# Attention in front of a Fourier mixer and an MLP: the product with V in 64-column halves, and the softmax's sums as a product of their own

## The chip, the cores and the metric

The kernel runs on one core of one Trainium2 chip. The metric is the device time of one execution in microseconds (us). The core has five engines that run side by side, each through its own instructions in order: TensorE (PE, matrix products), VectorE (DVE), ScalarE (ACT), GpSimd (POOL) and SyncE (SP, which here only issues DMA transfers).

## The reference

Eight batches, eight heads, 576 positions, head dimension 64, all in float32. Attention with a causal mask and a bias from cumulated sums comes first; its output goes, per batch as a 576 x 512 matrix, through a real part of a two-dimensional Fourier transform, a layer norm and an MLP of width 2048.

```python
scores = scale * (q @ k.T); bias = -(cum[:, None] - cum[None, :])
scores = where(causal, -1e9, scores + minimum(bias, 0)); scores -= max(scores)
attn = exp(scores); attn = attn / (sum(attn) + 1e-9)
x = attn @ v                       # per head: 576 x 576 times 576 x 64
u = x + real(fft(fft(x, axis=seq), axis=d_model))
un = (u - mean(u)) / sqrt(var(u) + 1e-6)
out = u + relu(un @ w_ch1) @ w_ch2
```

## The kernel before

Work goes in 32 **pairs** of heads (`NP`; four pairs make a batch). For pair `i` the function `maxes` finds the row maxima (products `pm`, line 459), `scores` forms transposed scores in PSUM (`ps`, lines 491 and 492: two products, high and low parts) and lets ACT write `P = exp(...)` to SBUF (line 495), after which POOL zeroes the masked corners (`affine_select`, lines 498 and 501). `P` of one head is a 128 x 1984 tile in five chunks of keys (`CH`, `POFF`): chunk 0 has 576 queries, chunk 1 has 448, and so on down to 64, because queries ahead of a key are masked.

`av` multiplies by V (line 523). Its operands are plain float32, not the one-pass `float32r` form that all other products but the transposes of `pmt` (line 471) use. Each head has two tiles of output columns, `pavA` (queries 0 to 255) and `pavB` (256 to 575), of 2 and 5 matmuls. The stationary operand is 128 columns wide: 64 columns of V of this head and 64 columns of ones, so 64 output rows are the head's result and the others the softmax's sums. ACT copies results to `x` (name `stage`) and the second head's sums to a row of `rows`; two DMAs per pair bring the sums to a tile `sums`. `recip` takes their reciprocals, writes them to DRAM (`rd`) and reads them back spread over partitions (`rb`); `finish` multiplies `x` by them. `recip` and `finish` of a pair are called an iteration after its `av`, except for the last pair.

The order is written by hand: in iteration `i`, `weave` mixes generators, always advancing the one whose yielded costs are the smallest share of its total. `av(i - 1)` (total `AV`), `maxes(i + 1)`, `low(i + 1)`, `high(i + 2)`, `scores(i)`, the Fourier products of the batch before (`pzs`, `pzc`, `pyc`, `pys`) and weight conversion are so interleaved. On PE this order is kept exactly. PSUM tiles of `maxes`, `av` and the transposes share five buffers of one tag. After the attention (line 622) come the last Fourier products and the MLP (`mlp_tile`, lines 183 to 198).

Of the kernel before, what the change touches and what calls it, by code (L numbers as in the profile page):

```python
# [8 lines left out]
F32 = mybir.dt.float32  # L9
# [10 lines left out]
S = 576  # L20
# [15 lines left out]
CH = [(0, 0, 576, 0), (128, 128, 448, 128), (256, 256, 320, 256), (384, 320, 256, 384), (448, 320, 256, 512)]  # L36
POFF = [0, 576, 1152, 1728, 1920]
# [4 lines left out]
def fused_kernel(ctx, tc, qkT, vA, sP, wP, tabD, tabS, corr, out):  # L42
    nc = tc.nc
# [4 lines left out]
    const = ctx.enter_context(tc.tile_pool(name="const", bufs=1))  # L48
# [6 lines left out]
    wD = dram.tile([NF, 128, 1024], F32, name="wD")  # L55
    uD = dram.tile([4, 128, NT], F32, name="uD")

    ident = const.tile([128, 128], F32, name="ident")
    make_identity(nc, ident)
    ones = const.tile([128, 128], F32R, name="ones")  # L60
# [40 lines left out]
    def load_w(pool, f):  # L101

        wh = pool.tile([128, 1024], F32R, tag=f"wh{f}", name=f"wh{f}")
        wl = pool.tile([128, 1024], F32R, tag=f"wl{f}", name=f"wl{f}")
        W[f] = (wh, wl)
        if f < NC:
            nc.sync.dma_start(out=wl.bitcast(F32), in_=wD[f])
        n = 512 if f < NC else WC
        for x in range(1024 // n):
            xs = slice(n * x, n * x + n)  # L110
            m = wl[:, xs].bitcast(F32) if f < NC else (yield from rounded(stage, f, x, nstage))
            nc.scalar.copy(wh[:, xs], m)  # L112
            yield 0.2 * n / 512
            (nc.vector if x * n < 512 else nc.gpsimd).tensor_sub(wl[:, xs], m, wh[:, xs].bitcast(F32))  # L114
            yield 0.2 * n / 512
# [101 lines left out]
    fft = fft_ctx.enter_context(tc.tile_pool(name="fft", bufs=1, side="right"))  # L217
# [7 lines left out]
    Aw = fft.tile([128, 577], F32, name="Aw")  # L225
    ZB = min(4, NB)
    z256 = [fft.tile([97, 3, ZB], F32R, name=f"z256{i}") for i in range(2)]
    rows = fft.tile([96, S], F32, name="rows")
    x256 = rows[:ZB]
    nc.vector.memset(Aw[:, 576:577], 0.0)  # L230

    def load_tables():
# [113 lines left out]
    attb = attb_ctx.enter_context(tc.tile_pool(name="attb", bufs=1, side="right"))  # L346
    psm = attb_ctx.enter_context(tc.tile_pool(name="psm", bufs=5, space=PSUM))
# [6 lines left out]
    cumD = dram.tile([3, 2, R, S], F32, name="cumD")  # L354
    cw = attb.tile([128, PW], F32, tag="P", name="cw", bufs=4)
    sp, zero, cum = (cw[:R, x * S:(x + 1) * S] for x in range(3))
    cumhl = attb.tile([128, PW], F32R, tag="P", name="cumhl", bufs=4)
    cw2 = attb.tile([128, PW], F32, tag="P", name="cw2", bufs=4)
    nc.sync.dma_start(out=sp, in_=sP)
# [63 lines left out]
    def low(i):  # L423

        st = sts[i]
        qk, qy, ky = st["qk"], st["qy"], st["ky"]
        pool = att if (NP - 1 - i) % 2 == 0 else atop
        q1 = pool.tile([128, 2, S], F32R, tag="q1", name="q1")
        k1 = pool.tile([128, 2, S], F32R, tag="k1", name="k1")
        nc.sync.dma_start(out=q1[0:64].bitcast(F32), in_=qy[64:128, :, 0:S].bitcast(F32))  # L430
        nc.sync.dma_start(out=k1[64:128].bitcast(F32), in_=ky[64:128].bitcast(F32))
        st.update(q1=q1, k1=k1)
        yield 1.0
        for h in range(2):
            nc.vector.tensor_sub(k1[0:64, h], qk[64:128, h], ky[64:128, h].bitcast(F32))
            yield 1.0
        for h in range(2):
            nc.gpsimd.tensor_sub(q1[64:128, h], qk[0:64, h], q1[0:64, h].bitcast(F32))  # L438
            yield 1.0
        va = attb.tile([128, 5, 192], F32, tag="va", name="va", bufs=2)  # L440
        nc.sync.dma_start(out=va, in_=vA[st["b"], :, :, st["j"]])
        st["va"] = va

# [35 lines left out]
    def scores(i):  # L479
        st = sts[i]  # L480
        qy, ky, q1, k1 = st["qy"], st["ky"], st["q1"], st["k1"]
        st["P"] = []
        for h in range(2):
            P = attb.tile([128, PW], F32, tag="P", name="P", bufs=4)
            st["P"].append(P)
            for c, (k0, q0, nq, qk) in enumerate(CH):
# [14 lines left out]
                        nc.gpsimd.affine_select(out=d5, in_=d5, pattern=[[1, 64]], compare_op=ALU.is_ge, fill=0.0, base=64, channel_multiplier=-1)  # L501
                    yield 2 * n / 2.4

    AV = 2 * 2700

    def av(i):
        st = sts[i]
        va = st["va"]
        x = attb.tile([128, S], F32, tag="stage", name="stage", bufs=3)
        r1 = rows[32 + 32 * (i % 2):33 + 32 * (i % 2)]  # L510
        sums = attb.tile([32, 36], F32, tag="sums", name="sums", bufs=2)
        for h in range(2):
            P = st["P"][h]
            vs = slice(64 * h, 64 * h + 128)
            for lo, n, tg in ((0, 256, "A"), (256, 320, "B")):
                p = psm.tile([128, 512], F32, tag="m", name="pav" + tg, bufs=5)
                cs = [c for c in range(5) if CH[c][3] < lo + n]
                for c in cs:
                    qk = CH[c][3]
                    a = max(lo, qk)  # L520
                    o = POFF[c] + a - qk
                    w = lo + n - a
                    nc.tensor.matmul(p[:, a - lo:n], va[:, c, vs], P[:, o:o + w], start=c == 0, stop=c == cs[-1])  # L523
                    if c == cs[-1]:
                        if h:
                            nc.scalar.copy(r1[:, lo:lo + n], p[0:1, :n])
                            nc.scalar.copy(x[64:128, lo:lo + n], p[64:128, :n])  # L527
                        else:
                            nc.scalar.copy(x[:, lo:lo + n], p[:, :n])
                    yield 4 * w / 2.4  # L530

            nc.sync.dma_start(out=sums[16 * h:16 * h + 16], in_=r1 if h else x[64:65])
        st.update(x=x, sums=sums)

    def recip(i):
# [29 lines left out]
    def call(fn, *args):  # L565
        yield 1.0
        fn(*args)
# [3 lines left out]
    weave([high(0), 1])  # L571
    cum_rows()
    weave([low(0), 1], [high(1), 1], [maxes(0), 1.0])
    weave([low(1), 1], [high(2), 1], [maxes(1), 1.0])
    mixing = None
    weights = convert_w(attb, 0, NC, 1)
# [8 lines left out]
    for i in range(NP):  # L585
# [3 lines left out]
        if i >= 1:  # L589
            streams.append([av(i - 1), AV * (0.95 if i % 4 == 1 else 1.0)])  # L590
        if 2 <= i + 1 < NP:
            streams.append([maxes(i + 1), MAXES / 0.7])
            streams.append([later(low(i + 1), i % 4 == 0), (6, 7, 4, 3)[i % 4]])
# [26 lines left out]
        if i >= 7 and i % 4 == 3:  # L620
# [5 lines left out]
    w0 = ctx.enter_context(pool("w0"))  # L626
    stage, nstage = attb, 1
    weave([later(call(recip, NP - 2), 2), 10], [later(call(finish, NP - 2), 4), 10], [av(NP - 1), AV], [mixing, FOURIER * 0.1], [norm, 6 * 0.4],
          [chain(weights, *[load_w(w0, f) for f in range(N0)]), 4 * N0 * 0.7 + 1])
    recip(NP - 1)  # L630
# [56 lines left out]
def chain(*gens):  # L687
    for g in gens:
        yield from g
# [6 lines left out]
def later(gen, n):  # L696
    for _ in range(n):
        yield 1.0
    yield from gen


def weave(*streams):

    for _ in mixed(*streams):
        pass
# [47 lines left out]
def _perm():  # L753
    import numpy as np

    p = np.arange(128)
    t2 = 512 - p
    t2[0] = 256
    return np.concatenate([p, 128 + p, t2, 384 - p])


def _layout(inputs):
    import numpy as np

    slots = [0, 1, 2, 3, 7, 6, 5, 4]
    perm = _perm()
    q, k, v, s = (inputs[n] for n in ("q", "k", "v", "s"))
    nb = q.shape[0]
    vs = v[:, slots].copy()
    vs[:, 4:] = vs[:, 4:, :, ::-1]  # L770
    vp = np.zeros((nb, NH, 640, HD), np.float32)
    vp[:, :, :S] = vs
    vp = vp.reshape(nb, 4, 2, 5, 128, HD)
    vA = np.ones((nb, 128, 5, 4, 192), np.float32)
    vA[..., 0:64] = vp[:, :, 0].transpose(0, 3, 2, 1, 4)
    vA[..., 128:192] = vp[:, :, 1].transpose(0, 3, 2, 1, 4)
    vA[:, 64:, 4] = vA[:, :64, 4]
    vA[:, :64, 4] = 0.0
    w1 = inputs["moe_w_ch1"][perm].reshape(4, 128, NF, 128)
    w2 = inputs["moe_w_ch2"][:, perm].reshape(NF, 128, DM)  # L780
    wP = np.concatenate([w1.transpose(2, 1, 0, 3).reshape(NF, 128, DM), w2], 2)
    wP = np.ascontiguousarray(wP).view(np.int64)
    tabD, tabS, corr = _tables()
    arrays = {
        "qkT": np.stack([a[:, slots].reshape(nb, 4, 2, S, HD).transpose(0, 1, 4, 2, 3) for a in (q, k)], 2).reshape(nb, 4, 128, 2, S),
        "vA": vA,
        "sP": s[:, slots].reshape(nb * NH, S),
        "wP": wP, "tabD": tabD, "tabS": tabS, "corr": corr,
    }
    return {n: np.ascontiguousarray(a) for n, a in arrays.items()}  # L790
# [22 lines left out]
```

## Time and profile before

| | us |
|---|---|
| three timed runs | 1425.22, 1425.87, 1433.48 (median 1425.87) |
| span of the profiled execution, first to last instruction | 1424.4 |
| PE, share of that span with a matmul under way | 1305.1 (92%) |
| DVE, ACT, POOL busy | 745.7, 539.3, 561.6 |

The profile is of one execution; its span stands 1.5 us below the median of the timed runs. A matmul's recorded duration includes its way through the array and overlaps that of the next, so starts, not durations, give its pace. One float32 product of line 523 makes two recorded matmuls, each with a weight load of its own (PEld).

### The profile page before, as it was taken

The numbers are of one execution on the slowest core, as the hardware profiler recorded it, in microseconds if no ns is written. First come the engines' busy times: TensorE is split into PE (matmuls) and PEld (weight loads), VectorE is DVE, ScalarE is ACT, GpSimd is POOL, SyncE is SP. The second block draws the span as 40 slices with busy tenths as digits, with TensorE's granted clock in tenths as the row PEclk, the third lists the DMA queues.
The fourth block names the chain that finished last, engine by engine and source line by source line (L and its number), as shares of the span: only waits on it lengthen the run. The fifth ranks groups of instructions, "written<-read, shape, count | busy, mean of one in ns | idle before, by whom it ended". The sixth has DMA issues, their size and how long they took to land.

```text
span 1424.4 us, 17997 instructions
## 1 busy us (share of the span) xinstructions
PE 1305.1 (92%) x6190; PEld 1068.7 (75%) x6190; DVE 745.7 (52%) x1684; ACT 539.3 (38%) x1211; POOL 561.6 (39%) x543
## 2 busy tenths in 40 slices
PE   4887979897988887997899999999999999999998
PEld 3766868686777676775688888888888888888886
DVE  6667677877777788799833233222332223322212
ACT  4775756676665656344321121211212112121110
POOL 6445465656546566565720402204022040123300
PEclk9998999999999997999899999999999999999999
DMA  8555556565655555433200000000000000000000
GB/s 214 156 159 144 163 149 180 158 168 159 159 161 144 166 149 163 162 123 121 79 8 30 31 30 15 15 30 31 30 15 15 30 30 30 15 16 0 30 0 30
DMA packets 78230, 125.05 MB, mean 88 GB/s; under 512 B 11256, under 2 KB 36249, under 8 KB 78139
## 3 DMA queue, kind: packets, MB, share of 16 engines
q1 hardware_dynamic: 75627, 119.83, 28.4%
q0 software_dynamic: 1696, 2.50, 0.9%
q10 hardware_dynamic: 816, 1.57, 0.3%
q8 instruction: 49, 0.80, 0.2%
q14 instruction: 42, 0.34, 0.1%
HBM read 76.85 MB, written 23.07 MB: 70 GB/s over the span
## 4 chain that ended last, share of the span: by engine, by line
PE 51%; DVE 7%; POOL 2%; DMA 1%; issue 1%; ACT 1%; SPq 0%; DVEq 0%; POOLq 0%; ACTq 0%
PE h L183 25%; PE acc L198 8%; PE acc L196 8%; PE acc L197 8%; POOL we L89 1%; DVE wm L88 1%; DVE we L83 1%; DVE wm L85 1%; DVE we L87 1%; DVE wl L114 1%; ACT wh L112 1%; DMA wl<-wD 0%; POOL wl L114 0%; DVE ucl L148 0%; DVE zl L188 0%
## 5 line engine op out<-in xcount | busy, mean ns | idle before, releaser
L188 DVE SCALAR_TENSOR_TENSOR zl<-h,zh 128x512 fp32r<-128x512 f32 x144 | 98.6, 686 | 405.5 <-ACT zh L187 405.4
L187 ACT ACTIVATE zh<-h 128x512 fp32r<-128x512 f32 x144 | 85.9, 596 | 530.1 <-PE h L183 530.1
L198 PE MATMUL acc<-zl,wh 128*128 128x512 f32 x576 | 227.5, 396 | 4.9 <-DVE zl L188 4.9
L196 PE MATMUL acc<-zh,wh 128*128 128x512 f32 x576 | 227.6, 395 | 1.0 <-ACT zh L187 1.0
L197 PE MATMUL acc<-zh,wl 128*128 128x512 f32 x576 | 226.8, 394 | 0.0
L523 PE MATMUL pavB<-P,va 128*128 128x320 f32 (+2 forms) x640 | 189.1, 389 | 9.5 <-ACT stage L527 8.9
L459 PE MATMUL pm<-KQ 128*128 128x256 f32 (+3 forms) x384 | 156.5, 427 | 44.4 <-DVE Mx L466 23.1
L495 ACT ACTIVATE P<-ps 128x320 f32<-128x320 f32 (+4 forms) x384 | 145.9, 393 | 110.5 <-PE ps L492 106.8
L491 PE MATMUL ps<-KQ 128*128 128x256 f32 (+2 forms) x384 | 154.1, 404 | 24.4 <-ACT P L495 14.0
L183 PE MATMUL h<-uch,wh 128*128 128x512 f32 x576 | 159.9, 398 | 8.3 <-ACT wh L112 8.3
L183 PE MATMUL h<-uch,wl 128*128 128x512 f32 x576 | 158.1, 396 | 0.8 <-DVE wl L114 0.8
L183 PE MATMUL h<-ucl,wh 128*128 128x512 f32 x576 | 156.9, 393 | 0.0
L466 DVE CUSTOM_DVE_ANT_0 trash<-pm,amask 128x128 bf16<-128x128 f32 (+3 forms) x256 | 123.5, 482 | 34.2 <-PE pm L459 16.9
L212 POOL TENSOR_TENSOR o<-o,w 128x512 f32<-128x512 f32 x32 | 41.8, 1305 | 252.3 <-issue 218.5
L183 PEld LDWEIGHTS h<-uch,wh 128*128 128x128 f32 x576 | 108.2, 190 | 35.9 <-ACT wh L112 12.1
L198 PEld LDWEIGHTS acc<-zl,wh 128*128 128x128 f32 x576 | 108.7, 189 | 32.0 <-DVE zl L188 6.9
L183 PEld LDWEIGHTS h<-uch,wl 128*128 128x128 f32 x576 | 109.2, 190 | 26.6 <-DVE wl L114 1.2
L196 PEld LDWEIGHTS acc<-zh,wh 128*128 128x128 f32 x576 | 108.6, 188 | 26.1 <-ACT zh L187 1.8
L183 PEld LDWEIGHTS h<-ucl,wh 128*128 128x128 f32 x576 | 108.9, 189 | 24.7
L197 PEld LDWEIGHTS acc<-zh,wl 128*128 128x128 f32 x576 | 108.6, 189 | 24.7
L459 PEld LDWEIGHTS pm<-KQ 128*128 128x128 f32 x384 | 78.4, 207 | 64.7 <-DVE Mx L466 30.2
L492 PE MATMUL ps<-q,k 128*128 128x256 f32 (+2 forms) x384 | 120.5, 316 | 3.1 <-POOL q L438 3.1
(140 smaller groups left out, 2066.9 us busy)
## 6 DMA issues: line engine op xcount, KB each, us to landing
qk<-in_qkT_dram SPq DMA_DIRECT2D x32, 576.0 KB
raw<-in_wP_dram SPq DMA_DIRECT2D x64, 256.0 KB
va<-in_vA_dram SPq DMA_DIRECT2D x32, 480.0 KB
q<-KQ SPq DMA_DIRECT2D x32, 288.0 KB
k<-KQ SPq DMA_DIRECT2D x32, 288.0 KB
rb<-rd SPq DMA_DIRECT2D x64, 144.0 KB
u<-uD SPq DMA_DIRECT2D x8, 1024.0 KB
out_dram<-o SPq DMA_DIRECT2D x32, 256.0 KB
```

Source lines behind the costliest of these rows:

```text
L183: nc.tensor.matmul(h[:, :n], a[:, j * 128:(j + 1) * 128], b[:, j, :n], start=i == 0, stop=i == 11)
L187: nc.scalar.activation(zh[:, :n], h[:, :n], AF.Relu)
L188: nc.vector.scalar_tensor_tensor(out=zl[:, :n], in0=h[:, :n], scalar=0.0, in1=zh[:, :n].bitcast(F32), op0=ALU.max, op1=ALU.subtract)
L196: nc.tensor.matmul(acc[j][:, :n], a[:, cs], y[:, :n], start=g == 0, stop=False)
L197: nc.tensor.matmul(acc[j][:, :n], b[:, cs], y[:, :n], start=False, stop=False)
L198: nc.tensor.matmul(acc[j][:, :n], a[:, cs], z[:, :n], start=False, stop=g == NF - 1)
L459: nc.tensor.matmul(p[:, :n], qy[:, h, 128 * c:128 * c + 128], ky[:, h, k0:k0 + n], start=True, stop=True)
L466: nc.vector.tensor_tensor_reduce(out=trash[:nq, :n], in0=p[:nq, :n], in1=amask[:nq, m0:m0 + n], scale=1.0, scalar=first if x else NEG, op0 ...
L491: nc.tensor.matmul(p[:, :n], ky[:, h, ksl], qy[:, h, a:a + n], start=True, stop=False)
L492: nc.tensor.matmul(p[:, :n], k1[:, h, ksl], q1[:, h, a:a + n], start=False, stop=True)
L495: nc.scalar.activation(P[:, o:o + a + n - lo], p[:, lo - a:n], AF.Exp, scale=0.125)
L523: nc.tensor.matmul(p[:, a - lo:n], va[:, c, vs], P[:, o:o + w], start=c == 0, stop=c == cs[-1])
```

## The change

In `av`, V of the two heads now stands side by side (`va` is 128 columns wide, without ones). For each chunk, head 0 multiplies with columns 0 to 63 of the array and head 1 with columns 64 to 127, one instruction after the other, into the two halves of the same PSUM tile. The sums are formed ahead of that by matmuls of their own (`psum`) with a 32-column stationary tile of ones, `on`; its second block of 32 columns has zeros in the upper half, for chunk 4, whose first 64 keys repeat others. There are four places for these: head 0 and head 1 for queries 0 to 395 (array columns 0 to 31 and 32 to 63) and for queries 396 to 575 (64 to 95 and 96 to 127). ACT copies `psum` in two pieces to `rsum`, and four DMAs per pair bring the rows to `sums`; `av` starts with a pause of 500 of its 4700 cost units. Matmuls of line 523 in the changed file are those of the sums, of line 540 those with V; other lines are shifted by 2.

```diff
+    on = const.tile([128, 64], F32, name="on")
+    nc.vector.memset(on, 1.0)
+    nc.vector.memset(on[0:64, 32:64], 0.0)
...
-    rows = fft.tile([96, S], F32, name="rows")
-    x256 = rows[:ZB]
+    x256 = fft.tile([ZB, S], F32, name="rows")
...
-        va = attb.tile([128, 5, 192], F32, tag="va", name="va", bufs=2)
+        va = attb.tile([128, 5, 128], F32, tag="va", name="va", bufs=2)
...
-    AV = 2 * 2700
+    AV = 4700
+    CUT = 396
+    SUM = [(0, (0, CUT)), (0, (CUT, S)), (1, (CUT, S)), (1, (128, CUT)), (2, (CUT, S)), (2, (256, CUT)), (3, (CUT, S)), (3, (384, CUT)), (4, (512, S))]
...
         x = attb.tile([128, S], F32, tag="stage", name="stage", bufs=3)
-        r1 = rows[32 + 32 * (i % 2):33 + 32 * (i % 2)]
         sums = attb.tile([32, 36], F32, tag="sums", name="sums", bufs=2)
+        yield 500
+        p = psm.tile([128, 512], F32, tag="m", name="psum", bufs=5)
+        for c, (a, e) in SUM:
+            o = POFF[c] + a - CH[c][3]
+            low = e <= CUT
+            z = a if low else a - CUT
+            for h in range(2):
+                g = 32 * h if low else 64 + 32 * h
+                nc.tensor.matmul(p[g:g + 32, z:z + e - a], on[:, 32 * (c // 4):32 * (c // 4) + 32], st["P"][h][:, o:o + e - a], start=c == 0, stop=c == (3 if low else 4))
+            yield 4 * (e - a) / 2.4 * 0.55
+        r = attb.tile([128, CUT], F32, tag="rsum", name="rsum", bufs=2)
+        nc.scalar.copy(r[0:64], p[0:64, 0:CUT])
+        nc.scalar.copy(r[64:128, 0:S - CUT], p[64:128, 0:S - CUT])
         for h in range(2):
-            P = st["P"][h]
-            vs = slice(64 * h, 64 * h + 128)
-            for lo, n, tg in ((0, 256, "A"), (256, 320, "B")):
-                p = psm.tile([128, 512], F32, tag="m", name="pav" + tg, bufs=5)
...
-                    nc.tensor.matmul(p[:, a - lo:n], va[:, c, vs], P[:, o:o + w], start=c == 0, stop=c == cs[-1])
-                    if c == cs[-1]:
-                        if h:
-                            nc.scalar.copy(r1[:, lo:lo + n], p[0:1, :n])
-                            nc.scalar.copy(x[64:128, lo:lo + n], p[64:128, :n])
-                        else:
-                            nc.scalar.copy(x[:, lo:lo + n], p[:, :n])
-                    yield 4 * w / 2.4
-
-            nc.sync.dma_start(out=sums[16 * h:16 * h + 16], in_=r1 if h else x[64:65])
+            nc.sync.dma_start(out=sums[16 * h:16 * h + 11], in_=r[32 * h:32 * h + 1])
+            nc.sync.dma_start(out=sums[16 * h + 11:16 * h + 16], in_=r[64 + 32 * h:65 + 32 * h, 0:S - CUT])
+        for lo, n, tg in ((0, 256, "A"), (256, 320, "B")):
+            p = psm.tile([128, 512], F32, tag="m", name="pav" + tg, bufs=5)
...
+                for h in range(2):
+                    nc.tensor.matmul(p[64 * h:64 * h + 64, a - lo:n], va[:, c, 64 * h:64 * h + 64], st["P"][h][:, o:o + w], start=c == 0, stop=c == cs[-1])
+                if c == cs[-1]:
+                    nc.scalar.copy(x[:, lo:lo + n], p[:, :n])
+                yield 4 * w / 2.4
...
-    vA = np.ones((nb, 128, 5, 4, 192), np.float32)
+    vA = np.empty((nb, 128, 5, 4, 128), np.float32)
...
-    vA[..., 128:192] = vp[:, :, 1].transpose(0, 3, 2, 1, 4)
+    vA[..., 64:128] = vp[:, :, 1].transpose(0, 3, 2, 1, 4)
```

The order on PE at the start of one iteration, in the second batch of pairs, before (`x3` would mean three equal rows in a line; the last size is the output's, partitions x columns):

```order
L491 MATMUL ps<-KQ_119 128x256
L492 MATMUL ps<-q_1540,k_1541 128x256
L459 MATMUL pm<-KQ_120 128x256
L491 MATMUL ps<-KQ_119 128x320
L492 MATMUL ps<-q_1540,k_1541 128x320
L523 MATMUL pavA<-P,va 128x128
L459 MATMUL pm<-KQ_120 128x384
L523 MATMUL pavB<-P,va 128x320
L459 MATMUL pm<-KQ_120 128x512
```

The same place on PE in the changed kernel, and on to the next products for the sums:

```order
L493 MATMUL ps<-KQ_122 128x256
L494 MATMUL ps<-q_1666,k_1667 128x256
L461 MATMUL pm<-KQ_123 128x256
L493 MATMUL ps<-KQ_122 128x320
L494 MATMUL ps<-q_1666,k_1667 128x320
L461 MATMUL pm<-KQ_123 128x384
L523 MATMUL psum<-P,on 32x396 x2
L461 MATMUL pm<-KQ_123 128x512
L493 MATMUL ps<-KQ_122 128x448
```

A single full-width product with V between two products of other streams has become a couple, one matmul for each head; the sums' couples come first, and the products with V (`64x256 x2` and so on) follow in the later part of the iteration. In the whole program the matmuls of lines 523 and 540 stand in 432 stretches between other work: 372 of them are one couple alone, 58 hold two or three couples of one kind, and two hold more; 448 matmuls with V have become 448 of half the width and 576 for the sums.

ACT in the same iteration, before, where copies of one head end (`rows`, `stage`):

```order
L526 COPY rows<-pavB 1x320
L420 CAST KQ_119<-qk 64x576
L69 CAST zc_2292<-pzc 96x258
L69 CAST zs_2294<-pzs 96x256
L527 COPY stage<-pavA 64x256
L527 COPY stage<-pavB 64x320
```

ACT in the changed kernel:

```order
L526 COPY rsum<-psum 64x396
L497 ACTIVATE P<-ps 128x64
L527 COPY rsum<-psum 64x180
L420 CAST KQ_124<-qk 64x576
L312 COPY yc<-pyc 128x290
L422 CAST KQ_124<-qk 64x576
L72 CAST De_2978<-Df 128x289
L497 ACTIVATE P<-ps 128x256
L542 COPY stage<-pavA 128x256
```

Six copies per pair have become four, and the sums' two now come before the results' two.

SP's queue of transfers near the end of the attention, before, where the last pair's sums are moved:

```order
L541 DMA rd<-sums 32x36
L532 DMA sums<-stage 16x1x36
L532 DMA sums<-rows 16x1x36
L130 DMA u<-uD 128x4x512
L544 DMA rb<-rd 64x576 x2
L541 DMA rd<-sums 32x36
```

In the changed kernel:

```order
L552 DMA rd<-sums 32x36
L529 DMA sums<-rsum 11x1x36
L101 DMA wD<-we 128x256
L530 DMA sums<-rsum 5x1x36
L529 DMA sums<-rsum 11x1x36
L555 DMA rb<-rd 64x576 x2
L530 DMA sums<-rsum 5x1x36
```

Two transfers have become four, and the fourth stands behind the two of `rb`.

More of the change, by code (lines that the diff above doesn't have):

```diff
@@ L509, in av @@
         x = attb.tile([128, S], F32, tag="stage", name="stage", bufs=3)
-        r1 = rows[32 + 32 * (i % 2):33 + 32 * (i % 2)]
         sums = attb.tile([32, 36], F32, tag="sums", name="sums", bufs=2)
-        for h in range(2):
-            P = st["P"][h]
-            vs = slice(64 * h, 64 * h + 128)
-            for lo, n, tg in ((0, 256, "A"), (256, 320, "B")):
-                p = psm.tile([128, 512], F32, tag="m", name="pav" + tg, bufs=5)
[L517 to L523, printed above, removed]
-                    if c == cs[-1]:
-                        if h:
-                            nc.scalar.copy(r1[:, lo:lo + n], p[0:1, :n])
-                            nc.scalar.copy(x[64:128, lo:lo + n], p[64:128, :n])
-                        else:
-                            nc.scalar.copy(x[:, lo:lo + n], p[:, :n])
-                    yield 4 * w / 2.4
-            nc.sync.dma_start(out=sums[16 * h:16 * h + 16], in_=r1 if h else x[64:65])
@@ new lines, in av @@
+        r = attb.tile([128, CUT], F32, tag="rsum", name="rsum", bufs=2)
+        nc.scalar.copy(r[0:64], p[0:64, 0:CUT])
+        nc.scalar.copy(r[64:128, 0:S - CUT], p[64:128, 0:S - CUT])
+        for h in range(2):
+            nc.sync.dma_start(out=sums[16 * h:16 * h + 11], in_=r[32 * h:32 * h + 1])
+            nc.sync.dma_start(out=sums[16 * h + 11:16 * h + 16], in_=r[64 + 32 * h:65 + 32 * h, 0:S - CUT])
+        for lo, n, tg in ((0, 256, "A"), (256, 320, "B")):
+            p = psm.tile([128, 512], F32, tag="m", name="pav" + tg, bufs=5)
+            cs = [c for c in range(5) if CH[c][3] < lo + n]
+            for c in cs:
+                qk = CH[c][3]
+                a = max(lo, qk)
+                o = POFF[c] + a - qk
+                w = lo + n - a
+                for h in range(2):
[3 more added lines that the diff above has]
+                yield 4 * w / 2.4
```

## The prediction

> **What bounds the kernel now.** The page's first lines say which engine to look at.
>
> ```profile
> span 1424.4 us, 17997 instructions
> PE 1305.1 (92%) x6190; PEld 1068.7 (75%) x6190; DVE 745.7 (52%) x1684; ACT 539.3 (38%) x1211; POOL 561.6 (39%) x543
> PE   4887979897988887997899999999999999999998
> ```
>
> PE is the busiest, but not evenly: the first half of the slices, which is the attention, has holes, the second half (MLP) none. The change touches only the first half, so I take the busy time of each engine in two stretches.
>
> ```profile
> core 0: us, PE busy (x) PEld busy (x) DVE busy (x) ACT busy (x) POOL busy (x), PEclk, DMA share, GB/s
> 75.00:530.00 455.00, 391.56 (x2225) 331.35 (x2223) 338.11 (x960) 288.66 (x720) 262.42 (x267) 0.95 0.56 157
> 800.00:1424.00 624.00, 618.77 (x2683) 503.22 (x2681) 172.49 (x230) 106.69 (x181) 127.57 (x96) 1.00 0.06 22
> ```
>
> In the attention PE is busy 86% of the time, with 63.4 us idle in 455; VectorE comes next with 74%. PE paces this stretch, but with holes. What ends these holes, in the same window:
>
> ```profile
> PE pm L459 <- DVE Mx L466: 22.4, 11, 5.5
> PE ps L491 <- ACT P L495: 11.6, 14, 2.2
> PE pavB L523 <- ACT stage L527: 8.5, 12, 1.6
> PE pm L459 <- DMA KQ<-cumD: 6.7, 4, 2.7
> PE ps L492 <- POOL q L438: 3.1, 3, 1.2
> PE ps L491 <- DMA KQ<-mt: 2.5, 5, 0.8
> PE pm L459 <- ACT stage L527: 2.4, 4, 0.7
> ```
>
> VectorE's maxima, ACT's exponentials and ACT's copies take turns; no engine other than PE sets the pace throughout. More work on PE is then partly swallowed by these holes, and less work on PE is partly lost in them. How long a pair takes comes from the one instruction that each pair has once:
>
> ```profile
> L471 PE MATMUL pmt<-ident,Mx x32: 270/272/374, 20.5 to 523.4; 128*10 128x128 f32 x32
> ```
>
> From the first to the last of 32 are 502.9 us, 16.2 us per pair; the idle share (63.4 of 455) is 2.3 us of that.
>
> **PE: the price of a column.** The next rows follow each other on PE.
>
> ```profile
> 303.86 0.70 PE L523 MATMUL pavB<-P,va 128*128 128x320 f32 x2
> 304.40 0.27 PE L471 MATMUL pmt<-ident,Mx 128*10 128x128 f32 x1
> 304.43 0.39 PE L491 MATMUL ps<-KQ 128*128 128x320 f32 x1
> 304.66 0.31 PE L492 MATMUL ps<-q,k 128*128 128x320 f32 x1
> 304.81 0.56 PE L315 MATMUL pys<-ssin,zs 96*128 96x290 f32 x3
> ```
>
> A float32 product of 320 columns (two recorded matmuls) takes 0.54 us from its start to the next: 1.69 ns per column, 0.84 per recorded matmul. The program's columns are counted from the loops. Before: per head 256 + 128 + 3 x 320 + 192 + 64 = 1600, so 3200 per pair, 102,400 in all, 173 us. After: 1600 columns for each of two heads with V and the same again for the sums: 204,800, which one after the other is 346 us. So the change has twice the columns, and everything hangs on how far products in different columns of the array run together. The hope in it would be two with V and four for the sums: a half and a quarter, 86 + 43 = 129 us. The order shows that four never meet in most places: 372 of the 432 stretches, with 167,288 columns, are one couple of two heads between full-width products. Perfect overlap of what stands together gives 171 us, 2 less than before. So even at its best PE's own work doesn't fall.
>
> Will a couple overlap perfectly? Each product is two recorded matmuls with weight loads of their own. In program order a couple is: first of head 0, second of head 0, first of head 1, second of head 1. The trace shows starts in program order, and the second of a product starts when the first is through (0.27 us for 320 columns, half of the 0.54). If head 1's first may start no earlier than head 0's second, one step is head 0 alone, one both, one head 1 alone: three steps instead of four, or of the two of perfect overlap. By this, stretches of one couple cost 167,288 x 1.69 x 3/4 = 212 us; in the others the steps overlap further (5 of 8 for two couples, with unequal widths about 0.66 over all), 37,512 x 1.69 x 0.66 = 42 us. Together 254 us: **81 us more** than before. No row here has two products in different columns, so the bounds are 171 (-2) and 346 (+173); I take the staggered one because it needs only order and dependence that the trace has. The Trainium skill ("TensorE: Matmul & The Clock Gate", part 3, "What overlaps and what doesn't") says that matmuls start and end strictly in program order, which is this staggering; its 2.38 times for three column tiles, taken as the same efficiency for two, would be 346 / 1.59 = 218 us, an estimate from that page, +45 us; no run here shows it.
>
> Each couple also needs head 1's first weights between two matmuls. How soon a matmul follows its load shows here:
>
> ```profile
> 307.20 0.30 PEld L523 LDWEIGHTS pavA<-P,va 128*128 128x128 f32 x2
> 307.25 0.65 PE L523 MATMUL pavA<-P,va 128*128 128x256 f32 x2
> ```
>
> 0.05 us for 128 columns; for 64 or 32 I take 0.03, between 0 and 0.05: 432 x 0.03 = **13 us** (0 to 22).
>
> Changing the width of the array's use, 432 times in and out: `pmt` above is such a change, 10 columns between wide ones. From its start to the second wide product after it are 0.26 us, of which the wide 320-column product takes 0.15 (304.66 to 304.81); the remaining 0.11 is what its own 128 columns in one recorded matmul take (128 x 0.84). So 0.01 us or less: **4 us**. For the upper bound I use how long an emptied array takes to fill:
>
> ```profile
> 305.99 0.28 PE L491 MATMUL ps<-KQ 128*128 128x256 f32 x1
> 306.10 0.28 PE L492 MATMUL ps<-q,k 128*128 128x256 f32 x1
> ```
>
> 0.28 us recorded, 0.11 from start to start: 0.17 us would show at each change if the array were emptied, 864 x 0.17 = 147 us. I take 4, from the nearer row, and keep 147 as a rival.
>
> Sum on PE: 81 + 13 + 4 = 98 us, 3.1 per pair. If PE's holes of 2.3 us per pair swallowed all they could, 26 would be left; if none, 98. PE's holes come from others' lateness, part of which (VectorE's maxima) vanishes when PE itself is later; part returns, since the other engines wait for PE in turn. I take two thirds: **+64 us**.
>
> **ACT.** The copies now:
>
> ```profile
> L529 ACT COPY stage<-pavB 128x320 f32<-128x320 f32 x32 | 13.6, 425 | 0.4
> L527 ACT COPY stage<-pavB 64x320 f32<-64x320 f32 x32 | 13.5, 420 | 0.1
> L526 ACT COPY rows<-pavB 1x320 f32<-1x320 f32 x32 | 13.3, 414 | 1.5 <-PE pavB L523 0.8
> L529 ACT COPY stage<-pavA 128x256 f32<-128x256 f32 x32 | 12.0, 376 | 0.0
> L527 ACT COPY stage<-pavA 64x256 f32<-64x256 f32 x32 | 11.8, 368 | 1.0 <-DMA sums<-stage 0.2
> L526 ACT COPY rows<-pavA 1x256 f32<-1x256 f32 x32 | 11.6, 362 | 0.8
> ```
>
> 75.8 us. Afterwards the two of 128 partitions stay (25.6), and two of 396 and 180 columns come, by the slope between 256 and 320 columns 0.48 and 0.30 us, 25 in all: 25 us less of ACT. PE waits for ACT 22.5 us in the window (11.6 + 8.5 + 2.4), so between 0 and 25 are won; with PE late by itself I take **-3**.
>
> **The masks of the second head.** Before, head 1's `P` is needed halfway through `av`; now the first couple needs both heads' masks (`affine_select`, line 498). At a late one of these (the rows of POOL, and of PE at the product that now stands just ahead of the first sums):
>
> ```profile
> 464.85 1.16 POOL L498 TENSOR_SCALAR_AFFINE_SELECT P<-P 128x512 f32<-128x512 f32 x1
> 465.15 0.44 PE L459 MATMUL pm<-KQ 128*128 128x384 f32 x1 [0.68 <-ACT stage L527]
> ```
>
> The mask ends at 466.0, where PE would be some 0.4 us past 465.15, having also lost the 0.6 us or so of products with V that stood ahead: about 1 us of PE waiting, with exponentials' products queued behind. That place comes once in a batch, where POOL is busy with the Fourier sums; elsewhere the mask is ready. **+3** (0 to 8).
>
> **The end of the attention.** The chain there:
>
> ```profile
> 556.14 0.41 ACT rows L526
> 558.43 3.65 DMA sums<-rows
> 562.38 0.37 DVE sums L539
> 562.75 3.21 DVE r L159
> ```
>
> The sums are ready some 4 us earlier when they come ahead of the products with V, but their last transfer now stands on SP behind the two of `rb`, and four must be issued, not two. Gain up to 4, loss up to 3: **-1**. In mid-attention two more transfers per pair on SP precede `rd` and `mt`; PE's waits for `mt` are 2.5 us in all, and the sums are ready before `mt`, so 0. `va`'s transfer shrinks by a third, behind other work. The MLP keeps its order: 0.
>
> Sum: 64 - 3 + 3 - 1 = +63 on the span of 1424.4: 1487; with the 1.5 us by which the span stands below the median, **1489**.
>
> **Rivals.**
> - *The couple overlaps perfectly*, and PE's columns cost the same as before (-2). Then 13 + 4 remain, 15 in all, two thirds on the path, 10; ACT's relief counts more, -8; masks and end +2: 1430, between 1412 and 1440: no change that can be told (1% is about what a measurement here can tell). For it: nothing in the trace forbids it; against it: a product's second half follows its first.
> - *Faster: ACT's relief comes through whole.* If couples overlap perfectly and their weights cost nothing, PE is even, and ACT's 25 us shrink the waits of `ps` and `pm`, by which 22.5 us of the window are held: 1426 - 25 - 2 + 2, about 1400. It decides once a couple takes at most two steps plus 0.01 us; at three steps PE's surplus is four times ACT's gain. Against it: the largest waits are VectorE's.
> - *No overlap at all* (the change doesn't do what it says): +173 + 4, of which nine tenths would come through with PE all but full: 1585.
> - *The array is emptied at each change of width*: with perfect couples -2 + 147, two thirds on the path, about 1520. The row of `pmt` speaks against it. The Trainium skill ("TensorEngine Tiling (Array Packing)", "Key Properties") says that changing the tiling mode drains the engine; the trace doesn't agree for `pmt`, whose entry and exit cost 0.01 us.
>
> **How the numbers follow.** Staggered couples 0.43 (1450 with the holes full, 1525 with none used), perfect 0.25, ACT's relief through 0.18, emptied 0.07, none 0.07. The likeliest gives 1489. The range leaves out half of the faster case below and the serial one above: 1402 to 1545. Faster by over 1%: 0.18; within 1%: 0.24 (nearly all of the perfect case); slower: 0.58.
>
> **What would show it.** Starts of the two heads' recorded matmuls: staggered means that head 1's first starts with head 0's second, and a couple of 320 columns takes about 0.8 us to the next product; perfect means 0.54, serial 1.07. Busy time of PE in the attention should rise from 86% above 90%, `pmt` come every 18 us instead of 16.2, and waits of PE for VectorE shrink. The MLP's starts should only be shifted. The forecast is wrong if couples take two steps, or if PE's surplus vanishes in its holes.

## The result and the profile after

The changed kernel takes 1525.1 us (median), the one before 1425.6; the ratio is 1.0667 (95% interval 1.0621 to 1.0714). The forecast was slower, 1489 us, in a range of 1402 to 1545. The profiled execution spans 1517.2 us, 92.8 more than before. The head of its page:

```profile
span 1517.2 us, 20371 instructions
PE 1429.9 (94%) x7342; PEld 1019.4 (67%) x7342; DVE 741.3 (49%) x1686; ACT 516.9 (34%) x1147; POOL 555.0 (37%) x543
PE   4998989998999999879879999999999999999998
```

PE's holes in the first half of the slices have become fewer, and that half is longer. By stretch (same columns as before), and by the one product that each pair has:

```profile
75.00:620.00 545.00, 513.68 (x3298) 294.11 (x3297) 341.52 (x979) 276.11 (x680) 267.66 (x278) 0.96 0.46 128
L473 PE MATMUL pmt<-ident,Mx x32: 270/272/415, 20.5 to 608.5; 128*10 128x128 f32 x32
```

PE is busy 94% of the attention instead of 86%, and a pair takes 588.0 / 31 = 19.0 us instead of 16.2: 85 of the 93 us are lost before the last `pmt`. What PE still waits for in that stretch:

```profile
PE pm L461 <- DVE Mx L468: 17.3, 8, 5.4
PE ps L493 <- DVE zc L73: 4.3, 6, 1.3
PE pmt L473 <- DVE Mx L468: 4.0, 4, 1.3
PE ps L493 <- ACT P L497: 2.5, 3, 1.2
```

VectorE's maxima hold PE less (17.3 us in 545, before 22.4 in 455), ACT hardly at all. PE has become the bound of the attention.

What a couple does is seen in the timeline (start, duration, how many records). One couple's first record, its first two, and its last two:

```profile
321.85 0.48 PE L540 MATMUL pavB<-P,va 128*64 128x320 f32 x1
321.85 0.49 PE L540 MATMUL pavB<-P,va 128*64 128x320 f32 x2
322.17 0.44 PE L540 MATMUL pavB<-P,va 128*64 128x320 f32 x2
```

Two records start at 321.85 and two at 322.17, 7 ns apart within each pair. So do the pairs of nearly all the 372 lone couples of the trace (5 to 8 ns). A record doesn't name its head; that a pair is one record of each head is read from the pace. The two halves of one product of 320 columns start 0.27 us apart in the kernel before, and four records one after the other would take 1.07 us, where the couple takes 0.69 from its start to the next product (322.54). So **the two heads run fully side by side**, not staggered. And then the whole stretch, with its neighbours:

```profile
321.61 0.31 PE L494 MATMUL ps<-q,k 128*128 128x320 f32 x1
321.85 0.76 PE L540 MATMUL pavB<-P,va 128*64 128x320 f32 x4
322.54 0.47 PE L493 MATMUL ps<-KQ 128*128 128x448 f32 x1
322.85 0.36 PE L494 MATMUL ps<-q,k 128*128 128x448 f32 x1
323.05 0.27 PE L473 MATMUL pmt<-ident,Mx 128*10 128x128 f32 x1
```

From 321.61 to 322.85 are 1.24 us. The full-width product of 320 columns takes 0.15 (304.66 to 304.81 before), a perfect couple 0.54, the product of 448 columns 0.20 (322.85 to 323.05): 0.89. **0.35 us are left over**: the price of one **stay**, a stretch in which only products of 64 or 32 array columns run, between full-width ones. The same subtraction at the 261 of 431 recorded stays where the neighbours allow it gives a median of 0.35, too. The weight loads show where it goes:

```profile
321.85 0.14 PEld L540 LDWEIGHTS pavB<-P,va 128*64 128x64 f32 x2 [0.20 <-issue]
322.54 0.19 PEld L493 LDWEIGHTS ps<-KQ 128*128 128x128 f32 x1 [0.49 <-issue]
```

The couple's load starts 0.24 us after the product ahead (321.61), where that product needs 0.15; the next full-width load starts at 322.54, 0.37 us after the couple's second half (322.17), which needs 0.27. Across a change of width nothing is loaded ahead here: no load starts until 0.09 us after the columns of the product ahead are through, and 0.10 us on the way out (over all stays both medians are 0.09). That fits an array that is first run empty, but the trace shows the loads, not the array. Then a load is waited for: the second half follows the first after 0.32 instead of 0.27 us, and the full-width product of 448 columns holds PE 0.31 instead of 0.20. With 432 stays at 0.35 that is an estimated 151 us; perfect couples give 2 back. The span grew by 93 us, 62% of these 149.

### The profile page after: what moved, and what is told of

It is laid out like the page before. It is cut to its first block, busy times and chain, and to the rows that moved or that the text cites. A ratio compares the mean times of both kernels' runs of the same rounds, so it can differ in the third digit from the quotient of the medians.

```text
span 1517.2 us, 20371 instructions
## 1 busy us (share of the span) xinstructions
PE 1429.9 (94%) x7342; PEld 1019.4 (67%) x7342; DVE 741.3 (49%) x1686; ACT 516.9 (34%) x1147; POOL 555.0 (37%) x543
## 4 chain that ended last, share of the span: by engine, by line
PE 72%; DVE 11%; DMA 3%; POOL 2%; issue 2%; ACT 1%; SPq 1%; DVEq 0%; POOLq 0%; ACTq 0%
PE h L186 23%; PE acc L199 8%; PE acc L201 8%; PE acc L200 8%; PE psum L523 5%; PE pm L461 5%; PE ps L493 4%; PE pavB L540 3%; PE ps L494 2%; PE pavA L540 2%; PE pyc L308 1%; POOL we L92 1%; DVE wm L88 1%; PE pys L317 1%; DVE k L437 1%
## 5 line engine op out<-in xcount | busy, mean ns | idle before, releaser
L461 PE MATMUL pm<-KQ 128*128 128x256 f32 (+3 forms) x384 | 149.8, 405 | 29.9 <-DVE Mx L468 18.0
L493 PE MATMUL ps<-KQ 128*128 128x256 f32 (+2 forms) x384 | 139.6, 365 | 19.4 <-ACT P L497 6.7
L461 PEld LDWEIGHTS pm<-KQ 128*128 128x128 f32 x384 | 75.3, 202 | 112.4 <-DVE Mx L468 48.9
L523 PE MATMUL psum<-P,on 128*32 128x180 f32 (+5 forms) x1152 | 137.5, 337 | 1.5 <-POOL P L500 1.1
L186 PEld LDWEIGHTS h<-uch,wl 128*128 128x128 f32 x576 | 109.8, 191 | 25.7
L493 PEld LDWEIGHTS ps<-KQ 128*128 128x128 f32 x384 | 75.9, 198 | 70.1 <-ACT P L497 23.7
```

What stands on the lines that cost most here:

```text
L186: nc.tensor.matmul(h[:, :n], a[:, j * 128:(j + 1) * 128], b[:, j, :n], start=i == 0, stop=i == 11)
L461: nc.tensor.matmul(p[:, :n], qy[:, h, 128 * c:128 * c + 128], ky[:, h, k0:k0 + n], start=True, stop=True)
L493: nc.tensor.matmul(p[:, :n], ky[:, h, ksl], qy[:, h, a:a + n], start=True, stop=False)
L523: nc.tensor.matmul(p[g:g + 32, z:z + e - a], on[:, 32 * (c // 4):32 * (c // 4) + 32], st["P"][h][:, o:o + e - a], start=c == 0, stop=c == ...
```

## The experiments

Theory A: the loss is the stays, in number, whatever runs in them. Theory B: it is in the couples, their loads and their number. Each ratio is to the kernel before, timed again beside the run (medians 1429 to 1431 us). The first three runs put small products into the kernel before, which has no couples at all:

```diff
+    nil = const.tile([128, 128], F32, name="nil")
+    nc.vector.memset(nil, 0.0)
...
+                    if c:
+                        nc.tensor.matmul(p[32:64, a - lo:a - lo + 12], nil[:, 0:32], ident[:, 0:12], start=False, stop=False)
                     nc.tensor.matmul(p[:, a - lo:n], va[:, c, vs], P[:, o:o + w], start=c == 0, stop=c == cs[-1])
+                    if not c:
+                        nc.tensor.matmul(p[32:64, a - lo:a - lo + 12], nil[:, 0:32], ident[:, 0:12], start=False, stop=False)
```

**narrow32**, as shown. Expected:

> The kernel before, with one small float32 product (12 columns, a zero stationary tile, added to the open sum) beside each of its 448 products with V, in array columns 32 to 63. Theory A (each stay of the array in a narrow form costs some 0.35 us of PE, because weights are not loaded ahead across the change and the array runs empty twice): 448 x 0.35 = 157 us on PE, six tenths of it on the path, about 1520 us. Theory B (the change of width is free, the loss of the changed kernel lies in its couples, their loads and their number): 448 x 0.1 us for two small loads and one wide load that nothing hides, six tenths on the path, about 1450 us.

Measured: 1527.0 us, ratio 1.065 (1.061 to 1.0691). 448 small narrow products make the kernel before as slow as the change did. On its timeline:

```profile
307.87 0.28 PE L461 MATMUL pm<-KQ 128*128 128x256 f32 x1
308.07 0.23 PE L526 MATMUL pavB<-ident,nil 128*32 128x12 f32 x2
308.24 0.81 PE L527 MATMUL pavB<-P,va 128*128 128x320 f32 x2
308.64 0.58 PE L461 MATMUL pm<-KQ 128*128 128x384 f32 x1
309.06 0.28 PE L493 MATMUL ps<-KQ 128*128 128x256 f32 x1
```

From 307.87 to 309.06 are 1.19 us, of which the three others need 0.11 + 0.54 + 0.16 = 0.81 (256, 2 x 320 and 384 columns): 0.38 us for a stay that has next to nothing to compute (median over the 221 places that allow the sum: 0.36). That is theory A's time; theory B's was 1450. The small product's first load, which has to wait:

```profile
308.07 0.14 PEld L526 LDWEIGHTS pavB<-ident,nil 128*32 128x32 f32 x2
```

It starts 0.20 us after the product ahead (307.87), which needs 0.11.

**narrow0**: the same in array columns 0 to 31 (`p[0:32, ...]`). Expected:

> The same small products with 32 columns, but in array columns 0 to 31, where the transposes and the last Fourier product stand, which showed no price of a change. Theory A in the form that the place decides: like B in the run before, 448 x 0.14 us, six tenths on the path, about 1460 us. Theory A in the form that any width under 128 columns costs: about 1520 us. Theory B: about 1450 us.

Measured: 1521.4 us, 1.0635 (1.0563 to 1.0706). The same stretch takes 1.19 us here too (308.63 to 309.82): a float32 product in columns 0 to 31 costs the same as one in columns 32 to 63.

**wide**: the same over all 128 columns (`p[0:128, ...]`, `nil[:, 0:128]`). Expected:

> The same small products over all 128 columns: no change of width, but two wide loads of 0.11 us that a product of 12 columns doesn't hide. Both theories: 448 x 0.2 us on PE, six tenths on the path, about 1480 us. Above narrow0 by 20 us or so if that place is free; below narrow32 by 40 under theory A, above it by 30 under theory B.

Measured: 1478.8 us, 1.0322 (1.0291 to 1.0354), as expected. The same stretch:

```profile
307.40 0.28 PE L461 MATMUL pm<-KQ 128*128 128x256 f32 x1
307.52 0.28 PE L526 MATMUL pavB<-ident,nil 128*128 128x12 f32 x2
307.66 0.78 PE L527 MATMUL pavB<-P,va 128*128 128x320 f32 x2
308.04 0.58 PE L461 MATMUL pm<-KQ 128*128 128x384 f32 x1
308.45 0.28 PE L493 MATMUL ps<-KQ 128*128 128x256 f32 x1
```

1.05 us, so 0.24 (median 0.23) for the small product with its two wide loads: less than 0.38 although the loads are four times as wide.

**narrow0r**: narrow0 with float32r operands (`nil` of float32r, `ones` for `ident`), which asks why `pmt` had shown no price. Expected:

> The small products of narrow0 once more (32 columns, in array columns 0 to 31), but of float32r operands, like the last Fourier product with its 4 columns, and so one recorded matmul each. Theory A, with the float32 form as what makes a stay narrow: no empty array, only 448 x 0.1 us of a wide load that a short product doesn't hide, six tenths on the path, about 1455 us. If any narrow product empties the array: 1510 to 1520 us.

Measured: 1457.2 us, 1.0186 (1.0147 to 1.0225). On its timeline, here with a product of 320 columns ahead and one behind:

```profile
310.42 0.31 PE L461 MATMUL pm<-KQ 128*128 128x320 f32 x1
310.57 0.17 PE L526 MATMUL pavB<-ones,nil 128*32 128x12 f32 x1
310.60 0.79 PE L527 MATMUL pavB<-P,va 128*128 128x320 f32 x2
310.98 0.55 PE L493 MATMUL ps<-KQ 128*128 128x320 f32 x1
311.36 0.31 PE L494 MATMUL ps<-q,k 128*128 128x320 f32 x1
```

0.94 us, 0.10 more than 0.15 + 0.54 + 0.15 (median 0.12). The small product starts as soon as the one ahead is through (0.15), and its weights are loaded ahead, just after that one's start (310.42):

```profile
310.43 0.11 PEld L526 LDWEIGHTS pavB<-ones,nil 128*32 128x32 f32 x1
```

So a 32-column product of float32r pays no price of a stay. The row of `pmt`, a float32 transpose, behaves like this one and was no guide to float32 products. Both are one recorded matmul where a float32 product is two; whether the type or that makes the difference was not tried apart.

The next runs change the number of stays. **group3**: the changed kernel with a pair's sums in one stretch, and pavA's and pavB's products in one each.

```diff
-            yield 4 * (e - a) / 2.4 * 0.55
+        yield 1467
...
-                if c == cs[-1]:
-                    nc.scalar.copy(x[:, lo:lo + n], p[:, :n])
-                yield 4 * w / 2.4
+            nc.scalar.copy(x[:, lo:lo + n], p[:, :n])
+            yield 4 * sum(lo + n - max(lo, CH[c][3]) for c in cs) / 2.4
```

Expected:

> The changed kernel with all products for the sums of a pair in one stretch, and those of pavA and of pavB in one each: 96 stretches or so instead of 432, with the same products. Theory A: 336 x 0.39 = 131 us less on PE, and more overlap of the four groups; about 1425 us (1410 to 1445). Theory B (couples themselves, or the order that starts with both heads' masks, cost the time): still above 1490 us.

Measured: 1452.0 us, 1.0133 (1.0105 to 1.0162): most of the loss is gone with the stays, but 1.3% is left, 7 us over the top of the expected range.

**group2** (one stretch for the sums, one with V; one `yield 2667`), **group5** (`yield` after the fourth and ninth of the sums, after pavA, and after the second and fifth chunk of pavB) and **group3b** (one stretch for the sums; with V, `yield` after the second and fifth chunk of pavB) move the cuts. Expected:

> Like group3, but all products with V of a pair in one stretch: 64 narrow stays instead of 96. Theory A alone: 32 x 0.385 = 12 us less on PE than group3, 1440 to 1447 us. If the long blocks on PE, during which ACT and VectorE get nothing new, are what is left of the loss: 1452 us or more.

> The changed kernel in about five narrow stays per pair: the sums in two stretches, pavA in one, pavB in two. Theory A alone, from group3 with 64 x 0.385 = 25 us more on PE, six tenths on the path: about 1467 us. If long blocks are what is left of the loss in group3, shorter blocks give back as much: 1445 to 1455 us.

> Like group3 (sums of a pair in one stretch, products with V in two), but the two of V cut after the second chunk of pavB instead of between pavA and pavB, so 0.96 and 1.73 us long rather than 0.65 and 2.05. Stays alone: as group3, 1452 us. If the length of the longest block counts: 1440 to 1450, near group5 or below, since it has 64 stays fewer.

Measured: 1447.5 us, 1.0126 (1.0083 to 1.0169); 1443.3, 1.0096 (1.0067 to 1.0125); 1453.1, 1.0159 (1.0134 to 1.0184). Group2 came out at the upper end of what the stays alone would give (1447), group5 below both of its forecasts, and group3b at what the stays alone would give (1452). By their intervals only group5 and group3b are told apart. Group5, with about 160 stays, is not slower than those with 64 or 96, as theory A alone would have it, so what is left is not mainly the stays. Shorter blocks on PE may be why; group3b, with shorter blocks of V but the same stretch of sums, came out no better than group3, so the reason stays open. None beats the kernel before.

**halves** takes the sums' products out, so that PE has less to do than before the change: the division is by other numbers, copied from `P`.

```diff
-        p = psm.tile([128, 512], F32, tag="m", name="psum", bufs=5)
-        for c, (a, e) in SUM:
...
+        yield 1467
+        P0 = st["P"][0]
...
+        nc.scalar.copy(r[0:64], P0[0:64, 0:CUT])
+        nc.scalar.copy(r[64:128, 0:S - CUT], P0[64:128, 0:S - CUT])
```

> The changed kernel without the products for the sums (the rows that become the sums are copied from P instead, so the division is by other numbers; the rest is as in the change): the products with V in halves alone, about 200 narrow stays. Theory A: 200 x 0.385 = 77 us more on PE for the stays and 86 less for the columns, which the two heads share; about 1420 us (1405 to 1435). Theory B: couples cost, above 1450 us.

Measured: 1457.1 us, 1.0195 (1.014 to 1.025): a miss, 22 us over the top of the range that theory A gave, and in the range of theory B (above 1450). Three runs asked why (their sums are copied too). **halves2** puts its products with V into two stretches:

> The run halves (products with V in halves, none for the sums, the sums' rows copied from P) with the products with V of a pair in two stretches instead of six or seven: 64 narrow stays. On PE, 87 us less for columns than before the change and 25 more for stays: 62 us less in all. If PE paces the attention and gives time back as it takes it (six tenths): about 1390 us. If a lighter PE only waits more, for the maxima and for transfers, and is granted a lower clock for it, as the profile of halves suggests (busy the same 14.3 us per pair as before the change, idle 2.95 instead of 2.2, clock 0.90 instead of 0.95): 1420 to 1455 us.

Measured: 1455.1 us, 1.0176 (1.0146 to 1.0206). **halves_fill** adds work to PE, a useless product ahead of each `pm`:

> The run halves with a second, useless full-width float32r product of 256 columns ahead of each product pm, into the same tile, which pm then overwrites: 384 x 0.11 = 42 us of PE work, which keeps PE from resting. If PE's work paces halves: 42 x 0.6 = 25 us more, about 1480 us. If the half-rate spells of PE's clock that come with its idle time pace it: fewer of them, and no more than 1460 us.

Measured: 1458.1 us, 1.0188 (1.0158 to 1.0218). **halves_even** spreads its products with V over the iteration (`AV = 2980`, a pause of 313 and none of 1467):

> The run halves (no products for the sums) with its products with V spread over the whole iteration again: the pause ahead of them is a tenth of av's cost, not four tenths. The products and the narrow stays (about 200) are the same. If the place of the products with V in the iteration (late, with the sums ahead of them) is what holds halves at 1455 us whatever PE's work is: 1425 us or less. If both heads' masks, needed at once, or the narrow stays hold it: 1450 us or more.

Measured: 1451.7 us, 1.0157 (1.0124 to 1.019). The window from 75 to 530 us of halves, halves2, halves_fill and halves_even, in this order (length, PE, PEld, DVE, ACT, POOL busy, PE's clock):

```profile
75.00:530.00 455.00, 380.32 (x2156) 257.06 (x2153) 324.79 (x929) 264.99 (x649) 251.33 (x255) 0.90 0.52 142
```

```profile
75.00:530.00 455.00, 354.28 (x2125) 268.01 (x2123) 325.58 (x920) 260.82 (x645) 249.84 (x254) 0.87 0.52 141
```

```profile
75.00:530.00 455.00, 396.13 (x2476) 285.11 (x2475) 322.90 (x927) 264.49 (x650) 250.74 (x255) 0.95 0.51 142
```

```profile
75.00:530.00 455.00, 383.89 (x2144) 257.25 (x2141) 332.36 (x924) 263.77 (x650) 252.69 (x255) 0.88 0.52 142
```

PE is busy 354 to 396 us of 455, its clock is granted at 0.87 to 0.95, and the kernel takes nearly the same time (1452 to 1458). Neither fewer stays of the same couples (halves2) nor more work (halves_fill) moved it, so in these four PE's work, couples included, doesn't set the time of the attention. A better clock in halves_fill, which came together with more work, didn't show either, and the place of V's products changed little. These variants of the order with both heads at once end 22 to 28 us above the kernel before. What holds them there was not settled: the masks of both heads needed at once, and the other order of ACT's and SP's work, were not tried apart. The traces lean to the second. In this window none of the four lists a wait of PE for a mask, while PE's waits for the transfer of `mt` are 10.1, 13.7, 6.1 and 17.4 us (2.5 before) and those of `pm` for VectorE's maxima 29.6, 33.0, 25.7 and 19.9 (22.4 before).

## Why the prediction was right, and where it was not

The direction was right, and 92.8 us on the span stand against 63 forecast; the mechanism that was forecast is refuted, and its place was taken by one of the rivals, which had a chance of 0.07. That the time still lies in the range is luck: the range was made wide for other cases.

- **Columns.** Twice the columns, mostly in lone couples, so nothing to win even at perfect overlap: confirmed. The couples overlap perfectly, so the column term is -2, the lower bound, not +81. The step that failed is "head 1's first may start no earlier than head 0's second": the records come in two pairs 0.32 us apart, with the two of a pair 7 ns apart. Whether the chip or the way from program to chip orders them so is not seen in the trace. The prediction's other sign, about 0.8 us from a couple to the next product if staggered and 0.54 if perfect, could have misled: 0.69 was measured, because 0.15 us of the change of width lie inside.
- **Change of width.** 4 us were taken and 147 kept as a rival, from 0.17 us at each of 864 changes; measured are 0.35 us per stay in and out, 151 us. The step that failed is the row of `pmt`: it has few columns, but pays no price of a stay, and neither does narrow0r's 32-column product of float32r. The nearest row was of another kind, and the far bound was near the right price, in part by chance: of its 0.17 us at each change 0.09 and 0.10 are measured before a load starts, and the other 0.16 of the 0.35 are loads waited for, which it didn't have. The Trainium skill's rule that a change of tiling mode drains the engine ("TensorEngine Tiling (Array Packing)", "Key Properties") agrees with the trace of the changed kernel, where nothing starts for 0.09 us going in and 0.10 coming out. That rival's time, about 1520, is within 5 us of the measured one.
- **Head 1's weights between matmuls** (13 us): wrong as put. The two heads' loads start 7 ns apart; what isn't hidden is the load behind a change of width, part of the 0.35 us.
- **Two thirds of PE's surplus** were to reach the span: 62% do here (two thirds of 98 is 65, where 64 was entered); of narrow32's 448 x 0.38 = 170 us, the 96 by which its median exceeds the 1431.3 of the kernel before are 56%.
- **ACT.** 50.6 us of copies were forecast, and the rows after give 15.4 + 13.5 + 11.9 + 9.7 = 50.5. What part of that relief reached the span (3 us were forecast) can't be read off a trace in which PE is the bound:

```profile
L526 ACT COPY rsum<-psum 64x396 f32<-64x396 f32 x32 | 15.4, 480 | 26.4 <-PE psum L523 23.5 <-DMA raw<-in_wP_dram 1.7 <-DMA k<-KQ 0.9
L542 ACT COPY stage<-pavB 128x320 f32<-128x320 f32 x32 | 13.5, 423 | 1.1 <-PE pavB L540 0.9
L542 ACT COPY stage<-pavA 128x256 f32<-128x256 f32 x32 | 11.9, 372 | 3.3 <-PE pavA L540 3.3
L527 ACT COPY rsum<-psum 64x180 f32<-64x180 f32 x32 | 9.7, 304 | 0.8
```

- **Masks.** 3 us were forecast; PE's waits of the sums for POOL's masks are 1.5 us, in the last pair:

```profile
L523 PE MATMUL psum<-P,on 128*32 128x180 f32 (+5 forms) x1152 | 137.5, 337 | 1.5 <-POOL P L500 1.1
```

- **The end.** -1 was forecast; behind the last `pmt` the span has 8 us more (908.7 instead of 901.0). The last two pairs' products lie there, and the trace has 17 narrow stays of them there, by their price 17 x 0.35 = 6 us of PE; it was not tried apart.

The total is thus a refuted +81, an underrated 4 and 13 at the wrong place, in place of -2 and 151, with the share on the path right. The faster rival, that ACT's relief would come through whole, needed couples at no further cost; even with PE relieved (halves2) no time was won.

## What to carry to other kernels

Packing two products side by side is worth only what is left after the array's changes of width, 0.35 us for each stay here: put narrow float32 products of a step together, and count stays before columns. Fewer stays took the loss from 6.7% to about 1%, but never below the kernel before. Take the price of a new kind of work from a row of the same kind (operand type, transpose or not); where there is none, a far bound that rests on a mechanism deserves more than 7%. And work taken off PE in an interleaved stage may win nothing: with 26 us less of busy PE in the window halves2 took as long as halves.

## What the runs showed of the hardware

A float32 product with 12 output columns in 32 array columns costs 0.38 us between full-width ones in both places tried, one of float32r 0.10, and one of float32 over all 128 array columns 0.24. The load of the first starts 0.09 us after the columns of the product ahead are through (median, narrow32 and narrow0); in wide and narrow0r it starts 3 ns after that product's start. Two float32 products in the two halves of the array start and end within some 7 ns of each other. In the four halves runs PE's granted clock was 0.87, 0.88, 0.90 and 0.95 with PE busy 354, 384, 380 and 396 us of 455, without a clear difference in the kernel's time.
